# Reordering the start of a transformer block: conditioning, first attention chunk and load queue

## The chip, the core and the metric

The kernel runs on one core of one Trainium2 chip. The metric is the device time of one execution in microseconds; lower is better. Before the change it is 639.45 us, the median of 4 runs between 637.75 and 639.82 us.

The engines are named as the profile names them. PE is the matmul engine, PEld its weight load, DVE the vector engine, ACT the scalar engine, POOL the general engine, and SP the engine that does nothing but issue transfers. ACT and POOL issue transfers too (ACTq and POOLq in the profile).

## What is computed

One transformer block with conditioning: 2048 positions, width 576, 32 heads of 18 columns, an attention in which each position looks at 8 positions (itself and every second one before it), and a gated feed-forward of width 4608. Cut to what matters:

```python
mod = (silu(c) @ w_mod).reshape(1, 6, 1, 576)
sa, ca, ga, sb, cb, gb = mod[:, 0], ..., mod[:, 5]
h = layernorm(x) * (1 + ca) + sa
q, k, v = h @ wqkv                      # 32 heads of 18
logits[s, w] = q[s] . k[s - 2*w] * 18**-0.5        # w = 0..7, masked where s - 2*w < 0
x = x + ga * ((softmax(logits) @ v_gathered) @ wo)
h = layernorm(x) * (1 + cb) + sb
x = x + gb * (((h @ w_gate) * (h @ w_up)) @ w_down)
```

## The kernel before: the parts that the change touches

The 2048 positions are cut into chunks of 128 or 256 rows. The attention of a chunk (`project`, then `attend`) is interleaved with the feed-forward of the chunk before it (`gate_up`, later `down`); each of these is a generator that yields at marked places, and a pacer decides when it goes on. Only the first chunk has no feed-forward to hide behind.

```python
SIZES = [128, 128, 256, 256, 256, 256, 256, 256, 256]
DOWN = [[[0], [1], [2]], [[3, 4]], [[5, 6]], [[7, 8]]]    # passes of gate_up, grouped by down
FB = 4                                                    # a weight block is 4 tiles of 128 columns
KEPT = [2, 3, 4, 5]     # these 4 of the 9 blocks stay in wd's space during the first three passes
...
    xin = pool("xin", 12)
    ps_att = pool("ps_att", 2, space=PSUM)       # 2 banks' worth for attention
    ps_mlp = pool("ps_mlp", 3, space=PSUM)
...
    v_sb = once.tile([P, D], BF, name="v_sb")                 # one buffer
    nc.gpsimd.memset(wqk[64:, KT - 1, :], 0.0)
    nc.gpsimd.memset(wo[64:, KT - 1, :], 0.0)
...
    load_x(0, nc.scalar)
    ... c_row loaded on nc.sync
    wmA = wm_tile()                                           # 2 buffers of this kind
    load_rows(nc.sync, wmA, w_mod[:, 0:2 * D])
    load_rows(nc.sync, wqk, A_wqkv[:, 0:2 * D])
    load_rows(nc.sync, wv_raw, A_wqkv[:, 2 * D:3 * D])
    nc.sync.dma_start(vd[0:HALO, :], zrow[:])
    load_x(1, nc.scalar)
    load_x(2, nc.scalar)
    wmC = wm_tile()                                           # ga and gb
    ...
    wmB = wm_tile()                                           # sb and cb
    load_rows(nc.sync, wmB, w_mod[:, 3 * D:5 * D])
    for d in range(DH):                                       # 18 transfers
        nc.sync.dma_start(wo[r0:r0 + H, d // 4, :], ...)

    # silu(c) as a row of 5 x 128, then transposed to columns, then broadcast
    nc.vector.tensor_copy(c_f[:], c_row[:])
    nc.scalar.activation(e_f[:], c_f[:], ACTF.Exp, scale=-1.0)
    nc.vector.tensor_scalar_add(e_f[:], e_f[:], 1.0)
    nc.vector.reciprocal(e_f[:], e_f[:])
    nc.vector.tensor_tensor(sc_row[:], c_f[:], e_f[:], ALU.mult)
    nc.tensor.transpose(pc[:], sc_row[:], ident[0:KT, 0:KT])
    nc.vector.tensor_copy(sc[:], pc[:])
    nc.vector.tensor_copy(sc_bc[:], ...)

    def mod_columns(wm, vi):          # 60 matmuls with one moving column each
        pm = att([P, 2, KT], F32, "pm")
        ...
    def mod_row(wm, gi, dst):         # 5 matmuls of 512 columns and 5 of 64
        ...
    mod_columns(wmA, 0)
...
    def project(ci):
        ln_rows(x_tiles[ci])
        yield "hT"
        ln_cols(hT[:, :, 0:C], C, 0, act_only=ci == 1)      # transposes, scale and shift
        ...                                                  # 40 matmuls pq, 5 pr
        for j in range(C // P):
            yield f"v{j}"
            ...                                              # 10 matmuls pv, pvr
            nc.scalar.copy(v_sb[:, 0:512], pv[:])
            nc.scalar.copy(v_sb[:, 512:D], pvr[:])
            nc.scalar.dma_start(vd[r0:r0 + P, :], v_sb[:])   # v to memory, to be gathered

    def attend(ci, dst):
        load_x(ci + 2, nc.gpsimd)
        ...                              # load_vsh: gather of v from vd on nc.gpsimd
        ...                              # prod = q * shifted k (8 of them), lgT: sums per head
        yield "lgT"
        ...                              # softmax: dd, mx, ssum, attn
        if ci == 0:
            setup_late()                 # releases the set-up buffers, makes hh, o_sb, oT, outp
        ...                              # vsh * attn, added up to o_sb
        yield "oT"
        ...                              # transposes, pw = o @ wo, y, x_t
        ln_rows(x_t)
        yield "h2T"
        ln_cols(dst, C, 2)
...
    for _ in project(0):
        pass
    mod_row(wmC, 0, ga_bc)
    mod_row(wmC, 1, gb_bc)
    mod_columns(wmB, 2)
    for _ in period(0):                  # attend(0) interleaved with project(1)
        pass
```

The feed-forward weights are loaded in 9 blocks of 1.18 MB. In the first pass each block goes by once for only 128 rows of positions. A scheduler orders the instructions of each engine, except where the kernel fixes the order itself (`manual_schedule`; before the change that holds for PE in the later passes only).

Of the kernel before, what the change touches and what calls it, by code (L numbers as in the profile page):

```python
# [14 lines left out]
PE = mybir.EngineType.PE  # L15

P = 128
# [29 lines left out]
def kernel(  # L47
# [33 lines left out]
    vshp = pool("vshp", 3)  # L81
    ps_att = pool("ps_att", 2, space=PSUM)
# [39 lines left out]
    v_sb = once.tile([P, D], BF, name="v_sb")  # L122
    vd = dramp.tile([HALO + S, D], BF, name="vd")

    nc.gpsimd.memset(wqk[64:, KT - 1, :], 0.0)
    nc.gpsimd.memset(wo[64:, KT - 1, :], 0.0)
# [21 lines left out]
    c_row = sp.tile([KT, P], BF, name="c_row")  # L148
    nc.vector.memset(c_row[:], 0.0)
    nc.sync.dma_start(c_row[0:KT - 1, :], c[0, 0:(KT - 1) * P].rearrange("(m p) -> m p", p=P))  # L150
    nc.sync.dma_start(c_row[KT - 1:KT, 0:64], c[0:1, (KT - 1) * P:D])
# [4 lines left out]
    wmA = wm_tile()  # L156
    load_rows(nc.sync, wmA, w_mod[:, 0:2 * D])
    load_rows(nc.sync, wqk, A_wqkv[:, 0:2 * D])
    wv_raw = sp.tile([P, KT, D], BF, name="wv_raw")
    nc.gpsimd.memset(wv_raw[64:, KT - 1, :], 0.0)  # L160
    load_rows(nc.sync, wv_raw, A_wqkv[:, 2 * D:3 * D])
    zrow = sp.tile([HALO, D], BF, name="zrow")
    nc.gpsimd.memset(zrow[:], 0.0)
    nc.sync.dma_start(vd[0:HALO, :], zrow[:])
    load_x(1, nc.scalar)
    load_x(2, nc.scalar)
    wmC = wm_tile()
    load_rows(nc.sync, wmC[:, :, 0:D], w_mod[:, 2 * D:3 * D])
    load_rows(nc.sync, wmC[:, :, D:2 * D], w_mod[:, 5 * D:6 * D])
# [5 lines left out]

    c_f = sp.tile([KT, P], F32, name="c_f")
    nc.vector.tensor_copy(c_f[:], c_row[:])
    e_f = sp.tile([KT, P], F32, name="e_f")
    nc.scalar.activation(e_f[:], c_f[:], ACTF.Exp, scale=-1.0)
    nc.vector.tensor_scalar_add(e_f[:], e_f[:], 1.0)  # L180
    nc.vector.reciprocal(e_f[:], e_f[:])
    sc_row = sp.tile([KT, P], BF, name="sc_row")
    nc.vector.tensor_tensor(sc_row[:], c_f[:], e_f[:], ALU.mult)
    pc = att([P, KT], BF, "pc")
    nc.tensor.transpose(pc[:], sc_row[:], ident[0:KT, 0:KT])
    sc = sp.tile([P, KT], BF, name="sc")
    nc.vector.tensor_copy(sc[:], pc[:])
    sc_bc = sp.tile([P, KT, P], BF, name="sc_bc")
    nc.vector.tensor_copy(sc_bc[:], sc[:, :, None].to_broadcast([P, KT, P]))
# [3 lines left out]

    def mod_columns(wm, vi):
        pm = att([P, 2, KT], F32, "pm")
        for bi in range(2):
            for m in range(KT):
                for half in ((slice(0, P),) if m < KT - 1 else (slice(0, 64), slice(64, P))):
                    n = half.stop - half.start
                    for kt in range(KT):  # L200
                        nc.tensor.matmul(pm[half, bi, m:m + 1], lhsT=wm[kp(kt), kt, bi * D + m * P:bi * D + m * P + n],
                                         rhs=sc[kp(kt), kt:kt + 1], start=(kt == 0), stop=(kt == KT - 1))
        with hp():
            nc.vector.tensor_copy(modc[:, vi:vi + 2, :], pm[:])
            nc.vector.tensor_scalar_add(modc[:, vi + 1, :], modc[:, vi + 1, :], 1.0)

    def mod_row(wm, gi, dst):
        pa = att([P, 512], F32, "pa")
        pb = att([P, 64], F32, "pb")
        for dstp, c0, c1 in ((pa, 0, 512), (pb, 512, D)):  # L210
            for kt in range(KT):
                nc.tensor.matmul(dstp[:], lhsT=sc_bc[kp(kt), kt, :], rhs=wm[kp(kt), kt, gi * D + c0:gi * D + c1],
                                 start=(kt == 0), stop=(kt == KT - 1))
        nc.scalar.copy(dst[:, 0:512], pa[:])
        nc.scalar.copy(dst[:, 512:D], pb[:])

    mod_columns(wmA, 0)
# [53 lines left out]
    for b in ORDER[0]:  # L271
        if b in KEPT:
            load_gu(b, KEPT.index(b))
        elif state["next"] < GU_BUFS:
            load_next()
    load_wd(len(KEPT) * WDB, FT)

    def setup_mid():
        for t in range(2):
            nc.gpsimd.tensor_copy(wqr[:, :, t * 64:(t + 1) * 64], wqk[:, :, t * D + 512:(t + 1) * D])  # L280
        for kt in range(KT):
            nc.vector.tensor_copy(wv[:, kt, :].rearrange("p (d h) -> p d h", d=DH),
                                  wv_raw[:, kt, :].rearrange("p (h d) -> p d h", d=DH))
# [3 lines left out]
    def setup_late():  # L287
# [3 lines left out]
        late["o_sb"] = late_once.tile([P, CH // P, DP], BF, name="o_sb")  # L291
        late["oT"] = late_once.tile([P, KT, CH], BF, name="oT")
        nc.gpsimd.memset(late["o_sb"][:, :, D:], 0.0)
        late["gup"] = pool("gup", 2)
        late["outp"] = pool("outp", 2)
# [36 lines left out]
    def project(ci):  # L332
# [27 lines left out]
        nc.vector.tensor_copy(kT[0:64, KT - 1, HALO:HALO + C], pr[64:, 0:C])  # L360
        nc.vector.tensor_copy(kT[64:, KT - 1, HALO - DIL:HALO - DIL + C], pr[64:, 0:C])  # L361
        for j in range(C // P):
            yield f"v{j}"
            pv = att([P, 512], F32, "pv")
# [9 lines left out]
            nc.scalar.dma_start(vd[r0:r0 + P, :], v_sb[:])  # L374

    def attend(ci, dst):
# [3 lines left out]
        load_x(ci + 2, nc.gpsimd)  # L380
# [55 lines left out]
        if ci == 0:  # L436
            setup_late()
        o_sb, oT = late["o_sb"], late["oT"]
# [19 lines left out]
        for j in range(ST):  # L458
# [8 lines left out]
            y = late["outp"].tile([P, D], BF, name="y")  # L467
# [97 lines left out]
    for _ in project(0):  # L565
        pass
# [56 lines left out]
```

## Time and profile before

The whole span of the profiled execution is 637.8 us. This table cuts it where the stages change; the busy times are those of the trace in these windows.

| window, us | what runs | PE busy, us | DVE busy, us | DMA, GB/s |
|---|---|---|---|---|
| 0 to 56.3 | set-up, attention of chunk 0, projection of chunk 1 | 30.27 | 27.45 | 249 |
| 56.3 to 95 | feed-forward of chunk 0, all but its last block | 34.23 | 23.65 | 270 |
| 95 to 600 | everything else but the last `down` | 492.0 | 260.6 | 99 |
| 600 to 638 | end of the last `down` | 32.37 | 4.86 | 16 |

(The third row is the sum of five windows; its rate is their mean, weighted by length.) Row 488 of the kernel is the feed-forward's gate and up matmul, row 514 its down matmul; these two make the busiest groups of the profile, 244.7 us and 147.1 us of PE.

Two things help in reading. A line of the timeline gives start, length, engine, line of the kernel, what is written and read, how many instructions were merged, and in brackets how long the engine had been idle before and what released it. And a line of the waits names who waited for whom, with the total, the number of times and the longest.

### The profile page before, as it was taken

The page shows a single profiled execution, that of the slowest core. Times are in us where ns is not written, and L with a number is a line of the kernel's source. Part 1 is how long each engine was busy: PE and PEld are TensorE (multiplying, and loading weights), DVE is VectorE, ACT ScalarE, POOL GpSimd, SP SyncE. Part 2 cuts the span into 40 slices and gives each one's busy share as a digit, 9 for nine tenths or more (in the row PEclk, how much of TensorE's full clock was granted, in tenths as well). Part 3 has the DMA queues.
Part 4 walks back from the last instruction along what each step waited for, and adds up shares of the span by engine and source line. Part 5 has one row for each costly group of instructions (what it writes and reads, how often), then busy time and mean ns, then how long its engine had stood idle before and what let it go on. Part 6 is the DMA issues. An engine that isn't in the chain of part 4 may idle for free.

```text
span 637.8 us, 11635 instructions
## 1 busy us (share of the span) xinstructions
PE 588.9 (92%) x4810; PEld 362.3 (57%) x4810; DVE 316.6 (50%) x694; ACT 270.5 (42%) x500; POOL 53.0 (8%) x107
## 2 busy tenths in 40 slices
PE   1876979989999999999998999999999999999996
PEld 1554756766767776454444776453446773333675
DVE  3365755974856755483547542663537532121111
ACT  2335646555547224454665114644642024444200
POOL 4301010010010120100000010000000000000000
PEclk9977998998999999999999999999999999999999
DMA  8869873332771032354510140355501003442000
GB/s 269 252 214 292 264 245 79 120 121 79 244 242 51 20 113 93 94 149 152 186 52 2 56 131 20 99 162 168 180 7 39 20 15 110 139 137 65 1 20 19
DMA packets 60782, 75.23 MB, mean 118 GB/s; under 512 B 4842, under 2 KB 54010, under 8 KB 60730
## 3 DMA queue, kind: packets, MB, share of 16 engines
q1 hardware_dynamic: 51898, 48.55, 25.8%
q0 software_dynamic: 5952, 23.01, 10.2%
q10 hardware_dynamic: 2880, 2.95, 1.4%
q8 instruction: 37, 0.61, 0.4%
q14 instruction: 15, 0.12, 0.1%
HBM read 69.75 MB, written 4.74 MB: 117 GB/s over the span
## 4 chain that ended last, share of the span: by engine, by line
PE 55%; DVE 9%; issue 5%; ACT 4%; DMA 3%; SPq 0%; POOL 0%; POOLq 0%; DVEq 0%; ACTq 0%
PE pgu L488 28%; PE acc L514 15%; PE pgu L496 5%; DVE vsh L443 2%; PE pq L351 2%; PE lgT L409 2%; PE pw L463 2%; ACT gu L502 2%; DMA gm<-in_B_w_up_dram 1%; PE pv L367 1%; DMA vsh<-vd 1%; ACT xn L312 1%; DVE ln_stats L303 1%; DVE vsh L444 1%; DVE ssum L432 1%
## 5 line engine op out<-in xcount | busy, mean ns | idle before, releaser
L488 PE MATMUL pgu<-h2T,gm 128*128 128x512 bf16 (+2 forms) x1344 | 244.7, 332 | 4.4 <-DMA gm<-in_B_w_gate_dram 3.4
L502 ACT CAST gu<-pgu 128x1024 bf16<-128x1024 f32 (+2 forms) x216 | 147.1, 731 | 156.1 <-PE pgu L496 155.2
L488 PEld LDWEIGHTS <-gm 128*128 128x128 bf16 x1344 | 115.5, 99 | 113.1 <-issue 19.0
L514 PE MATMUL acc<-wd,hh 128*128 128x288 bf16 x1152 | 147.1, 286 | 0.0
L503 DVE TENSOR_TENSOR hh<-gu 128x512 bf16<-128x512 bf16 (+2 forms) x216 | 70.2, 333 | 150.8 <-ACT gu L502 150.0
L514 PEld LDWEIGHTS <-hh 128*128 128x128 bf16 x1152 | 111.2, 98 | 30.8 <-issue 2.6
L400 DVE TENSOR_TENSOR prod<-qT,kT 128x1280 bf16<-128x1280 bf16 (+1 forms) x72 | 46.1, 686 | 19.0 <-PE lgT L409 18.8
L351 PE MATMUL pq<-hT,wqk 128*128 128x256 bf16 (+1 forms) x360 | 46.1, 281 | 6.7 <-ACT hT L328 4.1
L443 DVE TENSOR_TENSOR vsh<-vsh,attn 128x2304 bf16<-128x2304 bf16 x32 | 42.6, 1353 | 14.0 <-DMA vsh<-vd 13.9
L387 POOL DMA_DIRECT2D vsh<-vd x32 | 24.0, 751 | 270.7 <-DVE vsh L444 122.4
L496 PE MATMUL pgu<-h2T,gr 64*128 64x512 bf16 (+2 forms) x336 | 43.8, 332 | 0.2 <-DMA gr<-in_B_w_up_dram 0.2
L351 PEld LDWEIGHTS <-wqk 128*128 128x128 bf16 x360 | 34.9, 109 | 15.4 <-issue 11.5
L488 PE MATMUL pgu<-h2T,wd 128*128 128x128 bf16 (+1 forms) x384 | 38.1, 242 | 1.5 <-ACT gu L502 0.8
L519 DVE TENSOR_TENSOR y<-acc,gb_bc 128x576 bf16<-128x576 f32 x16 | 12.1, 756 | 47.2 <-PE acc L514 47.1
L488 PEld LDWEIGHTS <-wd 128*128 128x128 bf16 x384 | 27.6, 99 | 8.0 <-issue 4.6
L303 DVE BATCH_NORM_STATS2 ln_stats<-x_t 128x6 f32<-128x288 bf16 x64 | 25.8, 439 | 6.9 <-DMA x_t<-in_A_x_dram 6.5
L312 ACT ACTIVATE xn<-x_t,ln_nmr,ln_rstd 128x576 bf16<-128x576 bf16 x32 | 27.6, 863 | 1.5 <-DVE ln_nmr L310 0.9
L496 PEld LDWEIGHTS <-gr 64*128 64x128 bf16 x336 | 10.1, 94 | 28.3 <-issue 24.9
L522 POOL DMA_DIRECT2D out_dram<-y x16 | 8.8, 548 | 204.0 <-DVE y L521 204.0
L463 PE MATMUL pw<-wo,oT 128*128 128x512 bf16 x80 | 21.8, 380 | 0.7 <-ACT oT L456 0.6
L367 PE MATMUL pv<-wv,hT 128*128 128x512 bf16 x80 | 21.9, 388 | 0.5 <-DVE kT L361 0.3
L444 DVE TENSOR_TENSOR vsh<-vsh 128x2304 bf16<-128x2304 bf16 x16 | 21.6, 1353 | 0.2
(105 smaller groups left out, 424.3 us busy)
## 6 DMA issues: line engine op xcount, KB each, us to landing
vsh<-vd POOLq DMA_DIRECT2D x32, 576.0 KB, 5.6
gm<-in_B_w_gate_dram SPq DMA_DIRECT2D x27, 512.0 KB, 3.8
gm<-in_B_w_up_dram SPq DMA_DIRECT2D x27, 512.0 KB, 5.2
wd<-in_B_w_down_dram SPq DMA_DIRECT2D x4, 1152.0 KB, 6.0
wm<-in_w_mod_dram SPq DMA_DIRECT2D x2, 1152.0 KB, 8.5
vd<-v_sb ACTq DMA_DIRECT2D x16, 144.0 KB, 2.5
out_dram<-y POOLq DMA_DIRECT2D x16, 144.0 KB, 2.0
wd<-in_B_w_gate_dram SPq DMA_DIRECT2D x4, 512.0 KB, 7.1
```

Source lines behind the costliest of these rows:

```text
L303: nc.vector.bn_stats(stats[:, j, hf, :], src[j][:, hf * 288:(hf + 1) * 288])
L312: nc.scalar.activation(xn[:, j, 0:D], src[j][:], ACTF.Identity, bias=nmr[:, j:j + 1], scale=rstd[:, j:j + 1])
L351: nc.tensor.matmul(pq[:, gi, 0:C], lhsT=wqk[:, kt, w0:w0 + P], rhs=hT[:, kt, 0:C], start=(kt == 0), stop=(kt == KT - 1))
L367: nc.tensor.matmul(pv[:], lhsT=hT[:, kt, j * P:(j + 1) * P], rhs=wv[:, kt, 0:512], start=(kt == 0), stop=(kt == KT - 1))
L400: nc.vector.tensor_tensor(prod[:, 0:nm, 0:C], qT[:, 0:nm, 0:C], kT[:, 0:nm, off:off + C], ALU.mult)
L443: nc.vector.tensor_tensor(vsh[:], vsh[:], attn[:, j, ws, None, :].to_broadcast([P, WG, DH, H]), ALU.mult)
L463: nc.tensor.matmul(pw[:], lhsT=oT[:, m, j * P:(j + 1) * P], rhs=wo[:, m, 0:512], start=(m == 0), stop=(m == KT - 1))
L488: nc.tensor.matmul(ps[:, t, 0:C], lhsT=gm[:, kt, t, fi * P:(fi + 1) * P], rhs=h2[:, kt, cs], start=(kt == 0), stop=False, skip_group_check ...
L496: nc.tensor.matmul(pss[hf][:, t, 0:C], lhsT=gr[rows, t, (i // 2) * P:(i // 2 + 1) * P], rhs=h2[rows, KT - 1, cs], start=False, stop=True, ...
L502: nc.scalar.copy(gu[:, :, 0:C], pss[hf][:, :, 0:C])
L503: nc.vector.tensor_tensor(hh[:, fo, cs], gu[:, 0, 0:C], gu[:, 1, 0:C], ALU.mult)
L514: nc.tensor.matmul(acc[:, q, 0:288], lhsT=hh[:, f, j * P:(j + 1) * P], rhs=wd[:, f, q * 288:(q + 1) * 288], start=(f == 0), stop=(f == FT ...
```

## The change

It rewrites the start and leaves the feed-forward as it was. Its parts are these:

- The order of PE, DVE and ACT in the start is fixed by hand. `mod_columns` and `mod_row` no longer run in one lump after the projection of chunk 0, but in places where PE waits for others.
- silu(c) is computed in columns (128 partitions x 5) after the transpose, not in rows (5 x 128) before it. The broadcast of it moves to POOL, as do two of the five reorderings of wv.
- Matmuls of zeros (`warm`) are added: 4 at the very start, 6 before the first `mod_columns`, 8 before the first feed-forward, so that PE has been at work when real work comes.
- `mod_columns` goes through the weight's rows in its outer loop, so that it can begin with the first half of wmA; wmA and wqk are loaded in halves.
- The x rows of chunks 1 to 5 are loaded from SP's queue, those of 3 to 5 between the feed-forward's blocks. The others are loaded from POOL, four chunks ahead instead of two.
- v_sb has two buffers, and from chunk 2 on v goes to memory from POOL's queue instead of ACT's.
- The zeros in the weights' unused rows are written by DVE instead of POOL, and o_sb, oT and outp no longer wait for the release of the set-up buffers.

Its core, with cuts marked:

```diff
+PE_DVE_ACT = {PE, mybir.EngineType.DVE, mybir.EngineType.Activation}
...
-    v_sb = once.tile([P, D], BF, name="v_sb")
+    vsbp = pool("vsbp", 2)
+    o_sb = once.tile([P, CH // P, DP], BF, name="o_sb")
+    oT = once.tile([P, KT, CH], BF, name="oT")
...
+    nc.vector.memset(zeros[:], 0.0)
+    for t in (wqk, wv_raw, wo):
+        nc.vector.memset(t[64:, KT - 1, :], 0.0)
...
+    def load_rows2(dst, src):
+        for k0 in (0, 2):
+            nc.sync.dma_start(dst[:, k0:k0 + 2, :], ...)
+        nc.sync.dma_start(dst[0:64, KT - 1, :], src[(KT - 1) * P:D, :])
...
-    load_x(1, nc.scalar)
-    load_x(2, nc.scalar)
+    load_x(1, nc.sync)                   # after wv_raw
     ... first half of wmC, wmB, wo
+    load_rows(nc.sync, wmC[:, :, D:2 * D], w_mod[:, 5 * D:6 * D])
+    load_x(2, nc.sync)
...
+    def silu_c():
+        nc.tensor.transpose(pc[:], c_row[:], ident[0:KT, 0:KT])
+        nc.vector.tensor_copy(c_f[:], pc[:])              # 128 x 5 from here on
+        ...
+        nc.gpsimd.tensor_copy(sc_bc[:], sc[:, :, None].to_broadcast([P, KT, P]))
...
     def mod_columns(wm, vi):
+        for kt in range(KT):
+            for bi in range(2):
+                for m in range(KT):
+                    ...
+    def warm(n):
+        for _ in range(n):
+            nc.tensor.matmul(pw[:, 0, :], lhsT=zeros[:, 0:P], rhs=zeros[:, 0:512], start=True, stop=True)
...
     for b in ORDER[0]:
         ... load block b
+        if b in (1, 3, 5):
+            load_x(3 + b // 2, nc.sync)
...
-            nc.scalar.dma_start(vd[r0:r0 + P, :], v_sb[:])
+            (nc.scalar if ci < 2 else nc.gpsimd).dma_start(vd[r0:r0 + P, :], v_sb[:])
...
-        load_x(ci + 2, nc.gpsimd)
+        if ci >= 2:
+            load_x(ci + 4, nc.gpsimd)
...
-    for _ in project(0):
-        pass
-    mod_row(wmC, 0, ga_bc)
-    mod_row(wmC, 1, gb_bc)
-    mod_columns(wmB, 2)
-    for _ in period(0):
-        pass
+    with tc.manual_schedule(engines=PE_DVE_ACT):
+        warm(4)
+        silu_c()
+        warm(6)
+        a0 = project(0)
+        next(a0)
+        mod_columns(wmA, 0)
+        for _ in a0:
+            pass
+        b0, a1 = attend_into_place(0), project(1)
+        go(b0, "lgT")
+        go(a1, "hT")
+        go(b0, "oT")
+        mod_row(wmC, 0, ga_bc)
+        go(a1, "q0")
+        mod_columns(wmB, 2)
+        go(a1, None)
+        go(b0, "h2T")
+        mod_row(wmC, 1, gb_bc)
+        warm(8)
+        setup_late()
+        go(b0, None)
```

(`go(g, label)` runs a generator up to its mark of that name.)

## The prediction, made before the changed kernel was run

> **What bounds the kernel now.** I read the slices of the page first, then busy time by windows, then PE's waits in the start, then PE's timeline there, and last the waits of SP's own queue. The slices (16 us each) show a PE that is nearly full from the eighth slice on and ragged before it, while DMA is the other way round:
>
> ```profile
> ## 2 busy tenths in 40 slices
> PE   1876979989999999999998999999999999999996
> ...
> PEclk9977998998999999999999999999999999999999
> DMA  8869873332771032354510140355501003442000
> ```
>
> So from about 110 us PE sets the time, and the change removes no feed-forward work. What can be won lies in the first 95 us. Columns of the next view: window, length, then busy us (instructions) of PE, PEld, DVE, ACT, POOL, granted clock, DMA share, GB/s.
>
> ```profile
> 0.00:56.30 56.30, 30.27 (x324) 23.12 (x325) 27.45 (x72) 18.07 (x50) 14.49 (x38) 0.91 0.80 249
> 56.30:95.00 38.70, 34.23 (x456) 25.88 (x456) 23.65 (x71) 21.93 (x60) 2.84 (x6) 0.94 0.86 270
> ```
>
> Before the first feed-forward matmul (56.29 us) PE idles 26.0 us of 56.3 and no other engine is full: a chain of dependent steps. After it PE idles 4.5 us and DMA is busy 86% of the time. PE's own timeline, at the places that count:
>
> ```profile
> 13.10 4.33 PE L201 MATMUL pm<-sc,wm 128*128 128x1 bf16 x60 [0.25 <-DMA wqk<-in_A_wqkv_dram]
> ...
> 19.97 4.49 PE L351 MATMUL pq<-hT,wqk 128*128 128x128 bf16 x38 [0.73 <-ACT hT L328]
> ...
> 32.09 3.55 PE L201 MATMUL pm<-sc,wm 64*128 64x1 bf16 x56
> 35.56 0.53 PE L409 MATMUL lgT<-prod,ind 128*32 128x128 bf16 x20
> ...
> 55.13 0.61 PE L321 MATMUL ln_pA<-ident,xn 128*128 128x128 bf16 x4 [4.84 <-ACT xn L312]
> ...
> 94.67 1.46 PE L488 MATMUL pgu<-h2T,gm 128*128 128x128 bf16 x12 [3.37 <-DMA gm<-in_B_w_gate_dram]
> ```
>
> The reader is to see three things. The chain begins only at 13.10 us, when silu(c) is ready (PE's longest wait, 12.7 us on sc_row). The second mod_columns (32.09 to 35.64) stands between the two halves of the logits of chunk 0, which everything after needs. And the last weight block of the first pass comes late, at 94.67. Why it is late, SP's queue tells:
>
> ```profile
> SPq L233 <- DMA vd<-v_sb: 11.6, 2, 6.4
> SPq L174 <- DMA vd<-v_sb: 7.2, 1, 7.2
> SPq L141 <- DMA wm<-in_w_mod_dram: 5.2, 1, 5.2
> ```
>
> SP's loads wait, in their order, on the completion of earlier transfers, among them ACT's writes of v, which wait for compute. By SP's timeline these stalls end at 48.28 and 82.18 us; in 80 to 85 us DMA is busy only 0.40.
>
> **What the Trainium skill says.** "TensorE: Matmul & The Clock Gate", Part 1: PE runs at half clock until it has been busy for a window of about 3.4 us, and falls back after an idle one. The trace agrees: 128-column matmuls start 107 ns apart at 20 to 24 us and at 56 to 60 us, 66 ns apart at 61 us; the granted clock is 0.50 in 55 to 60 us. It adds something the page does not say: while mod_columns runs (one moving column each), PE is "busy" but the clock still drops (0.50 in 37.5 to 42.5 us, right after the second one). "DMA: Bandwidth & Descriptors", Issuing engines are not separate DMA queues: all queues share the same 16 engines, so moving a load to another queue makes no bandwidth. The trace agrees: 246 to 352 GB/s in 50 to 80 us with SP and POOL together, share 0.79 to 1.08. What moves is who waits for whom.
>
> **The change, part by part.** I follow landmarks through the new order; durations are those of the trace before.
>
> Start. Loads move 329 to 353 GB/s from 2.5 us. wmA and the first x rows are 1.48 MB, so 4.3 us, landed near 7; before, x of chunks 1 to 3 (0.74 MB) was mixed in. silu(c) now hangs on c alone: c lands near 5, transpose, five small steps of 0.15 to 0.3 us with hops, ready near 6.7. Six warm matmuls of 512 columns at half clock (4 x 107 ns each) are 2.6 us and end near 7.5, so mod_columns runs 7.5 to 11.8 instead of 13.10 to 17.43: 5.6 us earlier. The warm matmuls win nothing here, as mod_columns lets the clock drop; I count pq at 107 ns as before.
>
> Projection of chunk 0. Transposes 0.6, hT 0.9 until pq can start, 40 x 107 ns = 4.3, pr 0.7: ends near 18.3 (before 24.99; one more us gained because the xn of chunk 1, 0.86 us, no longer sits between the hT steps on ACT). wqk needs 1.33 MB more, so it lands near 11.5, in time.
>
> Logits. Eight products take DVE 3.1 us (two groups of 1.56); with kT (0.9) before and lgT (0.5) after, near 23.3 instead of 36.09. This is the largest step, 12.8 us ahead: 5.6 and about 1 carried over, and about 6 because two mod_row (27.42 to 31.13) and mod_columns (3.55) are out of the way. POOL makes its kT copies before the gathers of v now, so these are issued near 24 and land 4.3 to 5.6 us later (the durations before), when attn is due: 23.3 + 0.9 + 4.1 = 28.3 to 29.
>
> Then PE becomes the chain. Behind the logits it does mod_row 1.8, transposes 0.6, mod_columns 4.0, pq 4.3, pr 0.7: near 36. The first product of chunk 1 needs that, and in DVE's order it stands before the last sum o_sb of chunk 0. So o_sb is near 37.2 instead of 47.75: of 12.8 us, 2.2 are given back. From o_sb to the first feed-forward matmul it was 8.5 us (47.75 to 56.29), now 9: v's matmuls and its copies (0.8) are ahead on PE and ACT, and gb_bc (0.8) is copied on ACT between xn and h2T. First feed-forward matmul near 46.3, 10.0 us earlier.
>
> Clock. mod_row (1.8) and 8 warm matmuls (1.7 to 3.4) fill the 4.84 us hole, so PE should be warm at 46. Before, it ran at half clock from 56.3 to 60.3: 2.0 us more.
>
> Weights. PE could then reach the last block of the first pass at 94.67 - 3.37 - 10.0 - 2.0 = 79.3. Will it be there? SP stalls once more on a write of v, that of chunk 1, which I put at 39.5; before that stall ended at 48.28, so the stream runs 8.8 us ahead. The third stall (5.2 us, of which DMA lost about 3) goes, for v of chunk 2 is written from POOL. But x of chunks 3 to 5, 0.88 MB, now stands between the blocks: 2.9 us at 300 GB/s. So the last block is there between 94.67 - 8.8 - 5.2 + 2.9 = 83.6 and, if a tighter stream also closes its other gaps, about 80.5. I take 82. The first pass is then limited by transfers, and 12.5 of the 15.4 us that PE could win are won.
>
> Rest. From there 543 us follow that the change hardly touches. After the 3.37 us wait the clock is 0.50 in 95 to 100 us, a loss of about 2 us; a shorter or split wait saves about half of it. Two buffers for v_sb remove ACT waits of 5.0 us in all (2), none on PE's path. Sum: 12.5 + 1.0 = 13.5; 639.45 - 13.5 = 626.0 us.
>
> **The rivals.** (1) PE-bound first pass: blocks arrive in time, all 15.4 us and the clock's 2 us are won: 622. For it speaks that blocks 2 to 7 never made PE wait before (all DMA waits after 56.3 us are the 3.4 and a 0.2); against it, DMA was at 0.79 to 1.1 all that time, and PE now asks sooner. (2) Transfer-bound first pass without relief: the stream needs as long after its last stall as before, 46.4 us from 48.28 to 94.67; with the stall's end at 41 and x in it, the last block comes at 87 or later and 7 to 8 us remain: 631. For it speaks that the third stall cost only part of its length; then faster PE only waits more. (3) The order by hand is worse than the scheduler's: DVE or PE is held behind something late (the product of chunk 1 before o_sb, mod_row waiting for the second half of wmC, which is now loaded behind wo), and the first matmul comes at 50: 630. Against it: each of these has slack of a few us in my times. (4) POOL's queue: v of later chunks waits there behind output writes, and gathers behind it. Before, POOL waited 204 us for output rows without PE noticing (its waits after 95 us add up to about 12 us, none on the gather), so I give it 1 us at most.
>
> **Range and chances.** 2% off is 626.7, just beside my point. Errors: 2 us in the first matmul, 2.5 in the last block, 1 in the rest; together about 3.5, times 1.3 for 8 in 10, somewhat more to the slow side as a hand-worked chain forgets waits: 620 to 632. Faster by over 2%: 0.54, within 2%: 0.45, slower 0.01, since nothing in the later 540 us gets longer.
>
> **What would show it.** Right: mod_columns near 7.5; logits' last lgT near 23; first feed-forward matmul at 45 to 48 with 66 ns spacing; a wait on gm or wd in the first pass, and its last block at 80 to 84; from there to the end about 542 us. Wrong: no such wait and the last block before 79.5 (rival 1); first matmul after 49 (rival 3); last block after 86 (rival 2); more than 545 us after it (rival 4).

## The result, and the profile after

The changed kernel takes 634.02 us (median of 11 runs, 632.40 to 638.55) against 639.85 us for the kernel before, timed beside it on the same chip (16 runs, 634.20 to 642.82). The ratio is 0.9927, 95% interval 0.9899 to 0.9955. The prediction said 626.0 us with a range of 620 to 632: too much gain, by 8 us. The profiled execution spans 630.5 us (before: 637.8).

The slices of the page of the changed kernel (16 us each): the fourth slice (47 to 63 us) is full now, where it was 6 tenths before; the sixth (79 to 95 us) is still at 7, with the clock at 7 and DMA at 6.

```profile
PE   6879978989999999999998999999999999999996
...
PEclk9998979899999999999999999999999999999998
DMA  9689966124670141445501130546501004541000
```

Busy time of the changed kernel by windows, up to its first feed-forward matmul and from there to the end of the first pass (window, length, then busy us and instructions of PE, PEld, DVE, ACT, POOL, granted clock, DMA share, GB/s):

```profile
0.00:46.20 46.20, 34.05 (x342) 22.84 (x343) 27.32 (x70) 18.39 (x50) 11.54 (x28) 0.96 0.81 244
46.20:95.90 49.70, 44.42 (x551) 31.82 (x550) 30.35 (x86) 29.33 (x77) 6.50 (x13) 0.90 0.84 266
```

The start shrank from 56.3 to 46.2 us, as planned. PE's timeline of the changed kernel, at the places shown before and at the ones that turned out to matter:

```profile
8.09 3.54 PE L209 MATMUL pm<-sc,wm 128*128 128x1 bf16 x60
...
13.93 4.43 PE L360 MATMUL pq<-hT,wqk 128*128 128x128 bf16 x40 [1.66 <-ACT hT L337]
...
23.05 1.51 PE L421 MATMUL lgT<-prod,ind 128*32 128x128 bf16 x20 [0.45 <-DVE prod L412]
...
46.18 0.71 PE L497 MATMUL pgu<-h2T,gm 128*128 128x128 bf16 x6 [0.70 <-ACT h2T L337]
...
80.34 0.61 PE L497 MATMUL pgu<-h2T,gm 128*128 128x128 bf16 x8 [1.93 <-ACT gu L511]
...
84.42 1.46 PE L497 MATMUL pgu<-h2T,gm 128*128 128x128 bf16 x12
...
91.14 0.84 PE L497 MATMUL pgu<-h2T,gm 128*128 128x128 bf16 x12
```

The first feed-forward matmul comes at 46.18 us, 10.1 us earlier than before (56.29). But the last block of the first pass starts at 91.14 instead of 94.67: only 3.5 us are left of the 10.1. No weight wait stands before blocks 7 (84.42) and 8 (91.14); what stands there is a wait on ACT at 80.34 and, from 84.42 on, matmuls that start 107 ns apart, half clock. SP's longest wait on a write of v in the first 95 us (11.6 and 7.2 us in all there before):

```profile
SPq L246 <- DMA vd<-v_sb: 4.1, 1, 4.1
```

The clearest account of the loss uses one landmark further on: the projection of chunk 3, whose last group (pr, five matmuls) is in every trace. From the first feed-forward matmul to it PE does the same work in both kernels, some 771 matmuls. (DVE does not: in the changed kernel 3.1 us more of its work falls into this stretch, 43.94 us instead of 40.86, and 3.4 us less behind it.) Before:

```profile
56.29:120.80 64.51, 59.06 (x771) 44.80 (x770) 40.86 (x111) 36.81 (x97) 4.45 (x10) 0.92 0.65 200
```

and in the changed kernel:

```profile
46.18:116.13 69.95, 62.37 (x772) 46.05 (x771) 43.94 (x116) 37.61 (x99) 7.25 (x14) 0.90 0.73 232
```

The stretch became 5.44 us longer: 3.31 us because the same matmuls took longer (clock), 2.13 us of idle PE. So 4.67 of the 10.11 us arrive at the projection of chunk 3; from there to the end it is 517.0 us before and 514.4 after. So part of what this stretch loses comes back behind it, and between two kernels that order their work differently its length shows more than the whole loses. I call the 64.51 and 69.95 us "the middle stretch" below; the experiments all act on it.

### The profile page after: what moved, and what is told of

The parts are those of the page before. It is cut to its first block, busy times and chain, and to the rows that moved or that the text cites. A ratio compares the mean times of both kernels' runs of the same rounds, so it can differ in the third digit from the quotient of the medians.

```text
span 630.5 us, 11644 instructions
## 1 busy us (share of the span) xinstructions
PE 593.4 (94%) x4828; PEld 362.3 (57%) x4828; DVE 316.2 (50%) x693; ACT 271.6 (43%) x502; POOL 59.6 (9%) x113
## 4 chain that ended last, share of the span: by engine, by line
PE 57%; DVE 10%; issue 6%; ACT 4%; DMA 1%; POOL 0%; POOLq 0%; DVEq 0%; ACTq 0%
PE pgu L497 29%; PE acc L523 15%; PE pgu L505 5%; PE pq L360 2%; DVE vsh L452 2%; PE pw L472 2%; ACT gu L511 2%; PE lgT L421 1%; PE pv L378 1%; DMA vsh<-vd 1%; ACT xn L321 1%; DVE ln_stats L312 1%; DVE ssum L444 1%; DVE vsh L453 1%; DVE hh L512 1%
## 5 line engine op out<-in xcount | busy, mean ns | idle before, releaser
L360 PEld LDWEIGHTS <-wqk 128*128 128x128 bf16 x360 | 34.7, 109 | 13.9 <-issue 9.6
L505 PEld LDWEIGHTS <-gr 64*128 64x128 bf16 x336 | 10.2, 94 | 27.9 <-issue 25.4
```

The source lines that it names most:

```text
L360: nc.tensor.matmul(pq[:, gi, 0:C], lhsT=wqk[:, kt, w0:w0 + P], rhs=hT[:, kt, 0:C], start=(kt == 0), stop=(kt == KT - 1))
L505: nc.tensor.matmul(pss[hf][:, t, 0:C], lhsT=gr[rows, t, (i // 2) * P:(i // 2 + 1) * P], rhs=h2[rows, KT - 1, cs], start=False, stop=True, ...
```

## The experiments

Three theories for the 5.4 us, and the rivals of each other:

- A, transfers: the stream of weights in the first pass cannot follow a PE that asks 10 us sooner.
- B, a later collision: the fourth gather of chunk 2 is now issued at 102.0 us, just when SP loads blocks 1 and 0 again (98.3 to 106.6 us); it lands at 109.4, and VectorE waits for it.
- C, order: which instruction stands before which. In the first three passes the scheduler decides it, and TensorE, ScalarE and VectorE work in order; one late value holds all that is behind it.

All times in this table are medians with the ratio to the kernel before, timed beside them; "middle" is the middle stretch of the profiled execution, and the first ff matmul is of the same one execution. The kernel before, timed anew beside each group of runs, gave medians of 638.30 to 639.85 us; by the intervals a difference between two rows is uncertain by some 2 to 3 us (an estimate).

| run | us | ratio (95%) | first ff matmul | middle |
|---|---|---|---|---|
| before | 639.85 | | 56.29 | 64.51 |
| changed | 634.02 | 0.9927 (0.9899-0.9955) | 46.18 | 69.95 |
| h1_reload_half | 632.21 | 0.9886 (0.9858-0.9914) | 47.02 | 67.29 |
| h0_first_half | 623.42 | 0.9760 (0.9735-0.9786) | 46.19 | 57.33 |
| before_first_half | 633.59 | 0.9923 (0.9898-0.9947) | 56.34 | 57.44 |
| v_all_pool | 634.08 | 0.9915 (0.9884-0.9946) | 48.94 | 67.56 |
| no_warm | 635.76 | 0.9949 (0.9923-0.9975) | 46.66 | 70.59 |
| order_by_program | 642.84 | 1.0088 (1.0054-1.0123) | 46.82 | 68.20 |
| order_by_program_half | 637.57 | 0.9996 (0.9973-1.0019) | 47.01 | 62.31 |
| late_loads_program | 637.29 | 0.9990 (0.9968-1.0013) | 47.70 | 61.62 |
| late_loads | 628.38 | 0.9842 (0.9804-0.9879) | 45.63 | 60.71 |
| x_late | 631.28 | 0.9874 (0.9841-0.9908) | 47.03 | 66.19 |
| wd_late | 631.89 | 0.9869 (0.9827-0.9911) | 45.97 | 63.42 |
| before_wd_late | 632.60 | 0.9896 (0.9867-0.9925) | 57.05 | 57.80 |
| gathers_behind | 634.17 | 0.9939 (0.9918-0.9960) | 45.55 | 67.94 |
| gathers_behind_late | 626.95 | 0.9819 (0.9795-0.9844) | 45.67 | 61.46 |
| warm_14 | 634.98 | 0.9928 (0.9897-0.9958) | 47.02 | 70.26 |
| late_loads_burden | 630.06 | 0.9840 (0.9800-0.9881) | 46.13 | 65.61 |
| after_burden | 638.29 | 0.9987 (0.9969-1.0005) | 46.83 | 74.29 |

**Half of the first pass's weights, in both kernels.** The gate half is loaded and stands in for the up half, so the up half of the weights is left out and the output is another one. In h0_first_half (the changed kernel) and before_first_half it is all nine blocks of the first pass (5.3 MB); in h1_reload_half only blocks 1 and 0 of the second pass.

```
-        for t, wsrc in enumerate((B_w_gate, B_w_up)):
+        for t, wsrc in enumerate((B_w_gate, B_w_up)[0:1 + full]):   # full = 0 for the blocks chosen
...
-                    ... lhsT=gm[:, kt, t, fi * P:(fi + 1) * P]
+                    ... lhsT=gm[:, kt, t * full, fi * P:(fi + 1) * P]
```

> The changed kernel, but the nine blocks loaded for the first pass bring only their gate half (the up matmuls of them read the gate half; 5.3 MB less is moved before 90 us, no matmul is left out; the scheduler moves some instructions of the first passes). Theory A (the last two blocks landed at 85.4 and 89.7 us, later than PE could have used them): these two land before 75, PE runs through to the end of the first pass without its idle 5 us and the half clock at 81 to 88, and the time falls by 4 to 8 us. Theory B: the end of the first pass may come sooner, but the same late gather then takes it back at about 105 us, and the time falls by 2 us at most. Theory C (in the first pass PE stands in order behind the layer norm of chunk 1): the idle time at 78 to 84 us stays, 0 to 2 us.

> The control: the kernel before the change, with the same half load of the nine blocks of the first pass (result not the reference's). In the trace of the kernel before the weights hold the first pass for 3.4 us ahead of block 8 and for 2 to 5 us ahead of blocks 4 to 7, with clock lost after them. Theory A (transfers took the lead that the new start won): the kernel before gains less than the changed one does from the same relief (10.7 us between the changed kernel and its half-load run), some 3 to 6 us, 633 to 636, and the difference between the two half-load kernels is 10 us, the lead at the first feed-forward matmul. If the kernel before gains the same 10 us (628 or less), the stream held both alike and the change lost its lead elsewhere.

> The changed kernel, but the two blocks that are loaded again in the second pass bring only their gate half (the up matmuls of these two blocks read the gate half too; 1.18 MB less is moved, and no matmul is left out). The order of the instructions of PE, DVE, ACT and POOL is the same. Theory B (the late gather: the lead of 10 us is kept until 108 us, and about 5 us of it are lost when the fourth gather of v of chunk 2, issued at 102.0, shares the transfer engines with these two reloads): the gather lands 1.5 to 3 us sooner, DVE's wait of 4.6 us before it shrinks to 2 or 3 us, PE's wait of 2.05 us and part of the half clock after it go, and the time falls by 2 to 5 us. Theory A (the first pass's weight stream takes the lead): no change beyond 1 us, since the first pass is the same. Theory C (the scheduler's order of the first pass): no change either.

With half the weights both kernels do the middle stretch in the same time, 57.33 and 57.44 us, and the whole lead of the start arrives: 10.2 us between the two medians (633.59 and 623.42). The kernel before gains 4.9 us from it (638.46 beside it), the changed one 10.6. That is theory A's pattern, and it shows that the new start is worth its 10 us where nothing in the first pass takes it back. It does not yet show for the changed kernel that bytes do it: with the smaller loads the scheduler also ordered the first passes anew, and more than a thousand of PE's 4828 instructions stand elsewhere. (In before_first_half only some 57 do, all behind 89 us; there the wait of 3.4 us for weights is gone. The waits of 2 to 5 us ahead of blocks 4 to 7 that its expectation names are not in the trace of before: from 56.3 to 95 us PE waits for weights 3.4 and 0.2 us.)

h1_reload_half keeps the order. VectorE's wait in 95 to 118 us, in the changed kernel:

```profile
DVE vsh L452 <- DMA vsh<-vd: 4.6, 1, 4.6
```

and with the half reloads:

```profile
DVE vsh L453 <- DMA vsh<-vd: 3.0, 1, 3.0
```

The gather still comes late, as it is issued at 103.4 us, but waits 1.6 us less; the middle stretch is 2.7 us shorter, the time 1.8 us. The wait shrinks as B had it; the gain in time (1.8 us by the medians, 2.6 by the ratios) is no larger than its uncertainty. So B is small at most.

**v of every chunk written from POOL, so that SP never waits for ACT's writes; and no warm-up matmuls.**

```
-            (nc.scalar if ci < 2 else nc.gpsimd).dma_start(vd[r0:r0 + P, :], v_sb[:])
+            nc.gpsimd.dma_start(vd[r0:r0 + P, :], v_sb[:])
```

> The changed kernel, but v of chunks 0 and 1 too goes to memory from POOL's queue, so that SP's loads wait for no write of v at all (the stall of 4.1 us that ended at 42.2 us goes). Theory A: the weight stream runs 3 to 4 us ahead, block 8 lands near 86 and the time falls by 2 to 4 us. Theory B: the lead at 100 us grows by at most 1 us and the late gather still costs what it cost: 0 to 1 us. A cost to both: the gathers of chunks 0 and 1 stand behind these writes on POOL, which is some 0.5 us each.

```
-        warm(4)
...
-        warm(6)
...
-        warm(8)
```

> The changed kernel without its 18 matmuls of zeros. By my prediction the first ten win nothing, as the clock drops under the one-column matmuls anyway: the first of those start near 6.9 instead of 8.1 us, so the start gains about 1 us; but the profile shows projection of chunk 0 at 107 ns with them, which must stay 107 ns without. The last eight were to keep the clock up for the first feed-forward; the trace has the first feed-forward matmuls at 107 ns until 48.9 us all the same, so leaving them out costs at most 1 us. Together: between -1 and +1 us. If warmth were worth what its author hoped, it would be 2 to 4 us slower.

v_all_pool ended the stream some 3 to 4 us earlier (DMA share 0.21 in 85 to 90 us, 0.84 in the changed kernel) and won nothing. It also brought the first feed-forward matmul 2.8 us later, so it tells little about A; but PE still stood idle 2.4 us in 80 to 85, without a weight wait, and block 8 began 44.8 us after the first feed-forward matmul (93.71 us), against 45.0 in the changed kernel, though the stream had ended: the first sign of C. Without warm-up the time is within its uncertainty of the changed kernel's (1.7 us above it).

**TensorE in the order of the program, with three streams.** The first passes are taken from the scheduler's hands on PE; then half weights; then, with all bytes, the x of chunks 3 to 5 and the last quarter of the down weights loaded behind block 8 instead of ahead of blocks 7 and 8. PE's order is the same in the three.

```
-AUTO = 3
+AUTO = 0
```

```
     def block_done(pi, b):
         ...
+        # once block 8 is issued, that is after block 1 of pass 0:
+            load_x(3 .. 5, nc.sync); load_wd(len(KEPT) * WDB, FT)
...
-        if b in (1, 3, 5):
-            load_x(3 + b // 2, nc.sync)
-    load_wd(len(KEPT) * WDB, FT)
```

> The changed kernel with TensorE's instructions in the order of the program from the first pass on, where the changed kernel leaves the order of its first three passes to the scheduler. Same bytes, same queue order on SP. Theory C (the scheduler's order puts TensorE and ScalarE behind the layer norm of chunk 1 at 76 to 84 us): those waits of some 5 us in all shrink, block 7 starts at its landing near 83 instead of 84.4 and block 8 near its landing of 89.7, clock no longer at half after 84; 628 to 632. Theory A (the weight stream sets the first pass): the same idle time comes back as waits on the gate and up weights of blocks 7 and 8, the last block still starts at 90 or later; 633 to 637. Third way: the order of the program loses more in the second and third passes than it wins in the first; over 637.

> The run before, and the nine blocks of the first pass load only their gate half, which stands in for the up half (5.3 MB of about 11 MB left out; the result is not the reference's). TensorE's order is the same, instruction for instruction, as in the run before, so the difference between the two is the weight stream alone, which the earlier half-load run could not say, because the scheduler had ordered it anew. Theory A: 8 us or more below the run before, last block of the first pass before 84 us. Theory C: 3 us or less below the run before, because the order was the cause and the half load had only brought another order.

> The changed kernel in the order of the program, and the x of chunks 3 to 5 (0.86 MB) and the last quarter of the down weights (0.58 MB), none of which the first pass reads, loaded behind block 8 instead of ahead of blocks 7 and 8. All bytes are still loaded and the result is the reference's. Theory A: blocks 7 and 8 land 4 us earlier (1.4 MB at some 350 GB/s), the last block of the first pass starts 3 to 4 us earlier than in the run in the order of the program, and the time is 2.5 to 4 us below it. Theory C: under 1 us below it. If the late loads collide with the gathers of chunk 2 at 85 to 95, the gain is taken back at about 105.

The order of the program loses 8.8 us, but behind the middle stretch: from the projection of chunk 3 to the end it takes 522.4 us, where the changed kernel takes 514.4 (the third way of the expectation). Within the middle stretch the two reliefs win 5.9 and 6.6 us, and 5.3 and 5.5 us of the time. I had announced this as a clean test of bytes. It is not quite one: PE's order was fixed, but ACT's and DVE's were not. PE's line in the order of the program:

```profile
87.77 1.01 PE L497 MATMUL pgu<-h2T,gm 128*128 128x128 bf16 x8 [3.29 <-ACT gu L511]
```

and with half the weights:

```profile
84.55 0.61 PE L497 MATMUL pgu<-h2T,gm 128*128 128x128 bf16 x8 [0.61 <-ACT gu L511]
```

These are not the same tile: at 87.77 it is the last of block 7, at 84.55 the second of block 8. The weights were there in both, as an earlier tile of the same block had run at 83.87 and 83.31. The 3.29 us are ACT's: the layer norm rows of chunks 1 and 3 stand ahead of the copy gu (87.37) in one ACT order, in the other gu (84.15) stands after the first row. So these three runs differ in bytes and in ACT's order.

**The late loads alone, and their parts**, with the first passes left to the scheduler; and the down weights' part in the kernel before.

> The changed kernel with its first passes left to the scheduler, and only the x of chunks 3 to 5 and the last quarter of the down weights (1.4 MB, none of it read in the first pass) loaded behind block 8 instead of ahead of blocks 7 and 8. No byte is left out. In the order of the program this was worth 5.5 us, as much as leaving out half of the first pass's weights (5.3 us). Theory A (the weight stream took the lead): blocks 7 and 8 land some 4 us earlier, the waits at 75 to 90 shrink, and the time falls by 5 to 10 us against the changed kernel, 624 to 629. Theory C (order): the layer norm of chunk 1 still holds TensorE for 5 us at about 80; 631 to 635.

> Of the late loads only the x of chunks 3 to 5 (0.86 MB), which the change itself had moved onto SP's queue ahead of blocks 7 and 8. The two blocks are issued 2.7 us earlier, but the down weights' last quarter stays ahead of them. If these loads were the damage the change did to its own stream: 3 to 6 us below the changed kernel, 628 to 631. If the last block's landing is set by what shares the engines at 75 to 90 us (the gathers of chunk 2), which is the same here: within 1.5 us of the changed kernel.

> Of the late loads only the last quarter of the down weights (0.58 MB) moved behind block 8: 1.6 to 2 us of the stream at 290 to 350 GB/s. Theory A: 1.5 to 4 us below the changed kernel, 630 to 632.5. Theory C: as the changed kernel, 633 to 635, or wherever the new order of the scheduler puts it.

> The control for the run before: the kernel before the change, with the last quarter of the down weights behind block 8. Its x loads are not on SP's queue. Half of the first pass's weights were worth 4.9 us to it, so 0.58 MB is worth 1 to 3 us: 636 to 638. If it gains as much as the changed kernel with all its late loads, the gain is not one that the change had made possible.

late_loads leaves nothing out and is 5.6 us faster than the changed kernel. Its parts are worth 2.7 us (x) and 2.1 us (down weights), with uncertainties as large. The kernel before gained 5.9 us from the down weights' part alone, where I had expected 1 to 3. So with that one line moved, the kernel before is as fast as the changed one, and the difference that the change makes beside it (632.60 and 631.89) is not measurable; only with the x loads moved as well is the changed kernel ahead. By the ratios the two parts are worth 3.4 and 3.7 us. late_loads, x_late and wd_late got new orders, so in them bytes and order are still mixed. before_wd_late is cleaner: up to 89 us PE's order is that of the kernel before (130 of some 4810 instructions differ, all later), and the wait of 3.4 us for weights is gone (0.2 us is left in 70 to 100).

**The gathers of chunk 2 behind block 8, the order untouched.**

```
-            nc.gpsimd.dma_start(vsh[:]..., src)
+            (nc.sync if ci == 2 and (j, hf) != (1, 1) else nc.gpsimd).dma_start(vsh[:]..., src)
```

> The changed kernel, and of the four gathers of chunk 2 the first three (0.59 MB each) go to SP's queue, where they stand behind the weights of block 8 instead of leaving POOL's queue at 75.8 and 80.5 us beside them. The order on TensorE, VectorE and ScalarE is the same, instruction for instruction, and so are the bytes. Theory A in its sharper form (blocks 7 and 8 took 10 to 12 us from issue to landing because these gathers shared the engines): block 8 lands 3 to 5 us earlier, near 85, the last block starts 2 to 4 us earlier, and the time falls by 2 to 4 us against the changed kernel, 630 to 632. If the gathers then come too late for the attention of chunk 2 (needed from about 100), the gain goes back there. Theory C (order): the layer norm of chunk 1 holds TensorE to 83.5 as before and the last block starts within 1 us of 91; 633 to 635.

> The same gathers behind block 8, on top of the late loads of x and the down weights; orders of the three computing engines as in the run with late loads alone. In that run blocks 7 and 8 had landed before TensorE wanted them, so theory A expects nothing more from the stream: within 1.5 us of the late loads, 627 to 630. If it falls by 2 us or more, the gathers were holding something else; if it rises, the gathers came late for chunk 2.

This leaves every instruction of PE, DVE and ACT where it was. The gate and up weights land 5.6 to 9.3 us after issue instead of 5.2 to 11.9; block 8's gate half, issued at 76.89 in both, is there at 85.2 instead of 88.8, and the last rows of its up half at 87.1 instead of 90.7. The gate half's issue (what, queue, size, us from issue to landing) in the changed kernel, then in gathers_behind:

```profile
gm<-in_B_w_gate_dram SPq DMA_DIRECT2D x1, 512.0 KB, 11.9
```

```profile
gm<-in_B_w_gate_dram SPq DMA_DIRECT2D x1, 512.0 KB, 8.3
```

In the changed kernel the last rows land 0.4 us before PE comes to the block, so there the weights are nearly late; in gathers_behind they land 3 us ahead. PE's timeline of gathers_behind:

```profile
79.47 0.61 PE L497 MATMUL pgu<-h2T,gm 128*128 128x128 bf16 x8 [1.93 <-ACT gu L511]
...
83.42 1.46 PE L497 MATMUL pgu<-h2T,gm 128*128 128x128 bf16 x12
...
90.02 0.84 PE L497 MATMUL pgu<-h2T,gm 128*128 128x128 bf16 x12
```

These are the same waits as in the changed kernel, 0.9 to 1.1 us earlier, 0.6 of which it had already at the first feed-forward matmul. The time is unchanged (634.17; the ratio is 0.9939 instead of 0.9927). So with this order, weights that land earlier gain nothing that can be measured: C holds PE. What holds it is on ACT's timeline of the changed kernel (start, us, then engine, line and operation; in brackets the idle time before and what ended it):

```profile
79.59 0.20 ACT L316 ACTIVATE ln_rstd<-ln_rstd 128x1 f32<-128x1 f32 x1 [3.79 <-DVE ln_rstd L315]
```

ACT stands 3.79 us before the norm of chunk 1, whose statistics VectorE finishes only at 79.5 (y, the residual and four bn_stats come first); the copies gu, which free PE's accumulators, are queued behind it and run at 79.93. On top of late_loads the moved gathers change the time by 1.4 us at most (626.95), as expected; this is the fastest version here, 0.9819 of the kernel before, and leaves nothing out.

**Bytes put back, the order untouched.** Four copies of chunk 2's hT (1.31 MB) to an unused place in memory, issued by POOL at about 60 us, under the order of late_loads and under that of the changed kernel.

```
         ln_cols(hT[:, :, 0:C], C, 0, act_only=ci == 1)
+        for k in range(4 * (ci == 2)):
+            nc.gpsimd.dma_start(junk[k], hT[:].rearrange("p k c -> p (k c)"))
```

> The kernel with the late loads, whose order of instructions stays the same, one by one, on TensorE, VectorE, ScalarE and SP, and four copies of chunk 2's normalized input to an unused place in memory (1.31 MB in all, extra work that nothing reads), which POOL's queue starts at about 58 us. They put back on the DMA engines, in the place where the changed kernel loads x, the bytes that the late loads had taken away. If the bytes themselves held the first pass (theory A, plain): blocks 7 and 8 land 4 us later, weight waits appear at 70 to 90 us, and most of the gain over the changed kernel goes: 632 to 635. If the gain came from the order that the scheduler chose when it was given earlier weights (theory C, with the stream acting through the scheduler): within 1.5 us of the late loads, 627 to 630.

> The changed kernel, in its own order on every computing engine and on SP, with the same 1.31 MB of extra copies. gathers_behind took 1.8 MB from the engines at 75 to 82 us and won nothing, so in this order blocks 7 and 8 have some slack. Theory A, plain: the stream is the bound, so 1.31 MB at 290 to 350 GB/s cost 3.5 to 5 us, 637 to 639. Theory C: a part is hidden in the slack, 0 to 2.5 us, 634 to 636.5.

PE's waits in 70 to 95 us, first late_loads_burden, then after_burden:

```profile
PE pgu L497 <- DMA gm<-in_B_w_gate_dram: 1.7, 1, 1.7
```

```profile
PE pgu L497 <- DMA gm<-in_B_w_gate_dram: 3.4, 1, 3.4
```

Now weights are waited for, and the middle stretch grows by 4.3 us under the order of the changed kernel (69.95 to 74.29) and by 4.9 under the good one (60.71 to 65.61). 1.31 MB at some 300 GB/s is 4.4 us. In after_burden 4.0 of the 4.3 us are idle PE, and the time grows by the same 4.3 us: the bytes cost their full length, where theory C had expected a part to vanish in slack. In late_loads_burden only 1.2 us are idle PE; 3.7 are slower matmuls (clock 0.50 in 85 to 90 us, after the weight wait), and the time grows by 1.7 us by the medians and not at all by the ratios, with an uncertainty above either: here part of the bytes does vanish, as theory C had it.

So A and C both hold in part. In the changed kernel two limits of nearly the same length meet at 84 to 91 us: the landing of blocks 7 and 8, and the order that puts PE behind the norm of chunk 1. More bytes cost at once; fewer bytes in the way under this order win nothing that can be measured; fewer bytes with the order that the scheduler then makes win 5.6 us. With about the same bytes, the order of late_loads needs 65.61 us for the middle stretch instead of 69.95. (It is not quite the same load: 1.31 MB of writes from POOL's queue stand for 1.44 MB of loads in SP's.) By the middle stretch the order would win 4.3 us, half of it clock, and the bytes 4.9; but the stretch behind gives part of it back, 516.2 and 517.8 us for late_loads_burden and late_loads where the changed kernel takes 514.4. In all the order wins 4.0 us by the medians and the bytes 1.7, by the ratios 5.6 and nothing. So the order carries a good part of what the late loads win; the split is not resolved beyond that. The direct test of C, the copies gu ahead of the norm in ACT's order with all else kept, was not run, and why the scheduler made the worse order for the changed kernel was not tried.

**More warm-up.**

```
-        warm(8)
+        warm(14)
```

> The changed kernel with 14 warm-up matmuls ahead of the first feed-forward block instead of 8, so that TensorE is busy for 1.4 us of the 2.2 us that it stood idle there. Clock theory (idle time after the warm-up lost the clock again): the first feed-forward matmuls run at about 60 ns instead of 107, the clock of 45 to 50 us rises from 0.71, and 1 to 1.4 us are won at the start of the first pass, which the weight stream then takes back: 632.5 to 634.5. If the first matmuls still run at 107 ns, the idle time was not the cause.

PE's timeline of warm_14:

```profile
45.75 0.40 PE L330 MATMUL ln_pA<-ident,xn 128*128 128x128 bf16 x4 [0.17 <-ACT xn L321]
...
48.41 1.19 PE L497 MATMUL pgu<-h2T,gm 128*128 128x128 bf16 x10
```

and of gathers_behind, which has the 8 warm-up matmuls and 2.2 us of idle PE after them:

```profile
46.93 0.73 PE L497 MATMUL pgu<-h2T,gm 128*128 128x128 bf16 x10
```

With 14 warm-up matmuls (42.39 to 45.58) the gap is nearly filled (0.17 and 0.71 us are left of it); ten matmuls still take 1.19 us, half clock. With the gap, in gathers_behind, they take 0.73, full clock, though PE's order is that of the changed kernel, which was at half clock there. So whether there is a gap does not decide it alone; the last section has what the traces show beyond that.

## Why the prediction was wrong

- **Start, projection, logits: right.** mod_columns 8.09 to 11.6 (predicted 7.5 to 11.8), pr ends at 18.9 (18.3), the last lgT runs from 23.05 to 24.56 (its end was put at 23.3), attn 28.92 to 29.35 (28.3 to 29). Two of its sums don't add up: behind 18.3 the terms named (0.9, 3.1, 0.5) give 22.8, not 23.3, and behind 23.3 the next ones give 34.7, not 36; PE was through at 34.6. So the landmarks fit within 1.5 us, which is as close as the working was.
- **PE becomes the chain: right.** o_sb ends at 36.7 (37.2), first feed-forward matmul at 46.18 (46.3).
- **Clock: wrong, small.** "PE should be warm at 46": in the profiled execution it ran at half clock from 47.1 to 50.5 us. That cost 1.2 us against gathers_behind, which did the same matmuls at full clock (4.54 us from the first of them, 3.32 there), where 2.0 was the loss before. The Trainium skill, "TensorE: Matmul & The Clock Gate", Part 1, says that the window that decides is free-running and that the number of cold matmuls varies from run to run; gathers_behind agrees, with the same order of PE and full clock. So the prediction could not count on a warm PE at this point.
- **Weights: this is the step that failed.** "The last block is there between 83.6 and 80.5. I take 82 ... 12.5 of the 15.4 us that PE could win are won." Of these 12.5 (94.67 - 82 is 12.7), 3.5 came at block 8. Three terms were wrong. The stall on v of chunk 1 ended at 42.19, not 39.5: the write took 4.5 us to land, where that of chunk 1 had taken 1.9 us before. The landings of blocks 7 and 8 had no term at all: up to 11.9 us after issue, beside three gathers of chunk 2, at a DMA share of 1.04 to 1.06. The trace of the kernel before shows the same collision (10.8 us for its block 8, issued at 83.86, beside the same gathers), and I had not read it; it moved forward with everything else instead of going away. So block 8's gate half is issued 7.0 us earlier and lands at 88.8, not at 82. And the limit of PE, "94.67 - 3.37 - 10.0 - 2.0 = 79.3", took for granted that PE's own path to block 8 shifts with its start. It does not: the path runs over ACT and the norm of chunk 1, in an order that the scheduler made anew, and reaches block 8 at 90 even where the weights wait for it (gathers_behind). I had read PE's timeline of before for DMA waits alone.
- **Rest: 543 us, "1.0": better.** From the last block to the end it is 539.4 us instead of 543.1. It hides a loss, the wait of 4.6 us for the fourth gather (B), which before was 0.3.
- **Sum.** Predicted 12.5 + 1.0; by the spans 3.5 + 3.8 = 7.3, by the medians 5.8.
- **Rivals.** (2), transfers without relief, came nearest (last block at 87 or later, 631), but the weight waits that it names were not there; it had part of the cause. (1), 622, is what h0_first_half shows (623.42): that arithmetic was right for a first pass without the two limits. (3), a bad order, I had looked for in the part ordered by hand; it was in the part left to the scheduler. (4) did not show.

The signs that I had listed don't fit together as any branch had them: "a wait on gm or wd in the first pass" was absent and the last block late.

## What to carry to other kernels

A lead won at the start is worth only what the stretch behind it can follow with; measure that by taking half of the stream's bytes out of both kernels before you add the lead up. When the end of a wait moves, follow each in-order engine on the new path, ACT's norm and copies as well as DMA, for a second limit of nearly the same length. Loads that the present pass doesn't read belong behind the ones it does; and where a scheduler sets the order, a moved load changes that too, so an experiment on bytes needs a form that leaves the order alone.

## What the runs showed of the hardware

- The clock of PE differs between executions with the same order on PE. In the middle stretch the matmuls of the changed kernel were busy 62.37 us, those of gathers_behind 58.84, with the same waits on ACT at about 80; as the slower matmuls also filled idle time, the stretch itself differs by 2.0 us (69.95 and 67.94). Part of the 3.31 us above may be of this kind. Half clock came in stretches of 3.4 us or a multiple: in the changed kernel 47.06 to 50.47 and 81.2 to 88.0 us, each after 3.4 us in which PE was busy 1.23 and 1.43 us; in gathers_behind only 81.9 to 85.3, after 3.4 us with PE busy 1.42. In gathers_behind the gap before the first feed-forward matmul fell on two such stretches, with PE busy 1.93 and 2.50 us, and the clock stayed full. But in warm_14 half clock (48.5 to 51.9) followed a stretch with PE busy 2.29 of 3.4 us. So where a gap falls against these stretches makes a difference, but a busy share that decides does not come out of these runs.
- Under a full stream single transfers slow down by two or more: a write of v (144 KB) took 4.5 us where that of chunk 1 had taken 1.9 before, and the gate and up loads (512 KB) up to 11.9 us, where those issued before 70 us took 4.1 to 6.0. The Trainium skill, "DMA: Bandwidth & Descriptors", Queues, rings and completion order, says that an engine takes packets from its queues in turn; the slow write beside weight loads queued ahead of it agrees.
